# A new hand-written order for the same operations of a fused delta-rule and gated-MLP kernel

## The chip, the core and the metric

The kernel runs on one core of one Trainium2 chip. The metric is device time in microseconds (us), from the first to the last work of one execution. Five instruction queues work side by side: TensorE (PE in the profile, its weight loads PEld), VectorE (DVE), ScalarE (ACT), GpSimd (POOL) and the sync engine (SP), which here does nothing but issue DMAs. Each queue runs its instructions strictly in the order in which they were written; an instruction that waits holds up everything behind it on its queue.

## The reference

Two stages follow each other. The first is a delta-rule recurrence over 768 positions for 4 batches of 8 heads, head size 48:

```python
k_n = k / (np.linalg.norm(k, axis=-1, keepdims=True) + 1e-06)
for t in range(S):
    y[:, :, t] = np.einsum('bhd,bhde->bhe', q[:, :, t], state)
    v_old = np.einsum('bhde,bhd->bhe', state, kt)
    state = state + bt[:, :, :, None] * np.einsum('bhd,bhe->bhde', kt, vt - v_old)
```

Its output, with the heads side by side (384 wide), goes into a gated MLP:

```python
h = np.maximum(x @ w_in, 0.0)                    # 384 -> 1024
u, v = h[..., :512], h[..., 512:]
v_n = (v - mean(v)) / np.sqrt(var(v) + 1e-06)
v_s = np.einsum('ts,bsd->btd', w_spatial, v_n) + b_spatial[None, :, None]
return (u * v_s) @ w_out                         # 512 -> 384
```

## The kernel before

**The recurrence in steps.** Positions are taken in chunks of 64, and 24 steps `s` cover them (12 for the first two batches, 12 for the others). Within a chunk the recurrence is solved with a triangular inverse. `prep(g)` makes the inverses for four steps at once: matmuls of the keys with themselves (`kk`, line 557), a transpose into a layout with one system a lane (L576), norms (L584 to L591), and an elimination whose column steps are small elementwise operations, on DVE for groups 0 and 1 (L630, L633), on POOL for groups 2 to 5 (L615, L620); L645 transposes the result back. `widen16` and `widen` (L678 to L704 and L709 to L727; PE groups `e16`, `f16`, `e4`) put the small inverses together to 64 by 64. Then `step(s)` runs the chain that carries the state: PE group `a` (state times keys), a subtraction on DVE (L782), PE group `b`, a copy on ACT (L810, tile `w`), PE group `c`, and the update of the state on DVE (L823, L825 in step 0). `kq` (L753, its mask L757) and `qs`, `pu` make the output, which ACT copies to tile `xs` (L841). `load(s)` fetches k, q, v and n of a step (L733); there are two buffers `bn`, so the loads of step s+2 wait for the reads of step s.

**From the recurrence to the MLP.** After each two steps `convert(J)` moves six small pieces of `xs` by DMA (L858) and splits it into a high and a low part, `xh` on ACT (L862) and `xl` (L863, here on DVE), so that three products in a fast format make up one of full precision. `mlp(J)` then feeds PE with chunks of large matmuls (`v`, `u`), and `gate(b)` with the spatial and the output product (`g`, `o`).

**Decoding the weights.** w_in and w_out arrive as 64-bit floats. `load_f64` (L444) decodes a block: one load (L449), a chain of bit operations on ACT and DVE (L455 to L468), and a product, a difference and a sum (L469, L470, L471) that may run on DVE or POOL. There are six blocks `win0` to `win5`, all of which the MLP's first chunks need, and four blocks `wout0` to `wout3` that are needed much later.

**The order.** Nothing is scheduled by a tool when the kernel is built. `Plan.add` collects some 2,370 operations, and `listed` (L166) yields them in the order that the string `ORDER` spells out, two letters an operation; `PICK` has a digit for each operation that may run on either of two engines. A pair of letters beyond the last operation (`QW`) stands for a filler: two matmuls of a constant (`mpos`), whose result nobody reads; it is left out where no PSUM bank is free. `manual_schedule` keeps that order on each engine. All instructions of SP have line L411, all matmuls L524.

```python
for k in range(0, len(text), 2):
    i = LETTERS.index(text[k]) * n + LETTERS.index(text[k + 1])
    yield (self.ops[i], list(self.ops[i].alt)[pick.get(i, 0)]) if i < len(self.ops) else (None, None)
```

Of the kernel before, what the change touches and what calls it, by code (L numbers as in the profile page):

```python
# [36 lines left out]

LETTERS = "0123456789ABCDEFGHIJKLMNOPQRSTUVWXYZabcdefghijklmnopqrstuvwxyz!#$%&()*+-./:;<=>?@[]^_{|}~,"
ORDER = (
    "0407090605000102030J0Y080A0B0KQW0@0*0[QW0D0]0^0_0E0C0L0+0G0|0-0.0/0F0H0I0;1N0<1OQW1Y0N2U0M1P0P2R0:2S2V21221C2XQW2a0Q"  # L40
# [3 lines left out]
    "3L1p5U5V1J3M233H3N8R262P3B1A5Z3O451B3P1i1L1t1X1M2w2x2L2yQW2z2!2#2$3C2%3T2&3~2v2Q2(2)3U2*2+QW2-2.3D5X5Y5a3V3W3X3,403E"
    "QW3a413Y2/2:2;2<2=2>5b4L3Z463b42435c5d4447482?QW4A5e5f5g5h5i5j2@492[2]2^2_4M4N3I8U3eQW4O3i4B3kQW4CQW3h8d3j3d3l3c3f3g"
    "4P4QF74H4S4D4T4FQW5l2{5k5n2|1s5o5p5q2}3m4E4V4R4U4X4W4Y4G4Z4a4c5r8S5s8V2~8T5t515u5v5w8W5x4d5y525z1u1j5!4I3n4b504J1v4m"
    "536U3.3/3:4l5#3o565$4k4f4n4j4i4K4e8a5%8X5&1w1x556V5(5)5*5+5-575.5/3u1y5:1z5;5<5=3v3p5B3q5859546M5A3w5C3;3<6N3=6O5>5D"
    "6T5?3?1!6P3@6Q6R3r6W3[3s3]3^1#3t5@5[5]5^5_5F6j6S5m6X1%5E5{5G5|6k5}6l1$1&3x3y3z3>4o5~1(4h5,3_6Y6f6g1)6m6Z7O4p6a606d6n"
    "61623{6b8Y6c8Z5H6e5I3!5J6o3}1*QW3#631+647W8b7P8c7Q8e4q4g6q7X7R4:4]6566676p1-7S6r68694^4;6t6$4_4<3$1.3%3|8h3&7T6A6s6B"
    "1:6C6D6E6F6G6u7l7U6v6w6&6h6%3(6x1;8f8g4=4{6y4>6!6#6i6)6+6.6-6*6/7m7n1/4r7o4s6H6I6z8i7Y7t7p7h7q1=6J6K7s7V3)8j7r4?4t7u"  # L50
    "7Z6L8l8m4w4|4x7a7b4y7i7j6(8k3*8n8o6:8p8q6;7c7f7d8s4z4!7g9T7e8r9U4u4#4v7v7&8u4}7x4~8v8w8x8y7w7y78798z4@4,9V9q7)7(7A8!"
    "8#9a8$9W9r4[7z8%8&9X7!7$7*9s7%7k7+7/7-9Y1<7#At6]7B8(8)1>AV8*8+6^6_6<9b9t7C9c4$8-4%9u9v4&6=6>6?9y9dAu6{6|7D8.9Z3+9z8/"
    "8:8;9f9e8t4(9g9wAv6}8<8=9h7.7:IA7;9x9m1?9i9j6@9k7<4)9l1@7F6[8>4*8?Aw9!7G7H7IA>1[8@7E9#6~Ax8[Ay9$A?7J9%7=7_8]8^9&9*A@"
    "6,9+708_7>9nAz9p9o1]1^8{1|9(7?A#A[A]4+1_9)A!A%7@7[7]7{7|7}7^A^8|8QE~9/9.9@9-9>A$9?711{7K7L7NE{7M9=9<9;A(A|8}A&1}8~1~"
    "A)8A8,1,90A*3-7291928BAXA;A.A/8CA+8I7~8JQW8K8L8D8E8M8N8FA_A}7320AYAb939[A-9]7,7475A~9495AWAcAZ8P4-A{7680A,96Ad97B0AF"
    "9^B1AGAHAIB28O8HB39_A:B48182AaQWA<B5B6Ae984.999A9B9C9D9{AJAKE|9,9|9}A0F1BC4/E}83E,A1A284A3Af9~AgQWF0G5Ai9E85QWA48G9F"
    "9GBEBD9HF4BBBAGDB9B7A5A7Aj9IAhQW9J9K9L86A6AM9MGPGQG6ANAOAPAQF5ARASF29N9OF6Ak9PBFA8QW9QQWF3F8FAF99RF}BGBdGOFBFCBeF~Bf"
    "GH87A9QWF,ALFDG0GI9S88BNBOG1G2G4AAFFFGGJAUBPBQG|GKG3FEABG}G7BRA=ACGLG8FHAl9:B8FIGEFJFKBSADBgG9BHAmGMFMFNGAApGBGRG~GC"
# [1064 lines left out]
```

## Time and profile before

| | |
|---|---|
| Time, three runs | 472.31 us median (469.68 to 477.03) |
| Time of the profiled execution | 471.3 us, of which the span of its instructions is 469.6 us |
| First chunk of the MLP on PE | 85.5 us after the start |
| Fillers on PE | 24 before 109 us, 8 behind it |

The span starts with the first instruction of the program. A busy time is the union of the instructions' times on an engine. The profile also gives the clock that TensorE was granted, 1.0 for 2.4 GHz and 0.5 for 1.2 GHz.

### The profile page before, as it was taken

The numbers are of one execution on the slowest core, as the hardware profiler recorded it, in microseconds if no ns is written. First come the engines' busy times: TensorE is split into PE (matmuls) and PEld (weight loads), VectorE is DVE, ScalarE is ACT, GpSimd is POOL, SyncE is SP. The second block draws the span as 40 slices with busy tenths as digits, with TensorE's granted clock in tenths as the row PEclk, the third lists the DMA queues.
The fourth block names the chain that finished last, engine by engine and source line by source line (L and its number), as shares of the span: only waits on it lengthen the run. The fifth ranks groups of instructions, "written<-read, shape, count | busy, mean of one in ns | idle before, by whom it ended". The sixth has DMA issues, their size and how long they took to land.

```text
span 469.6 us, 21728 instructions
## 1 busy us (share of the span) xinstructions
PE 427.7 (91%) x9736; PEld 379.4 (81%) x9736; DVE 248.5 (53%) x558; ACT 230.6 (49%) x546; POOL 236.4 (50%) x371
## 2 busy tenths in 40 slices
...
GB/s 273 219 209 25 99 49 125 154 47 57 131 154 139 138 165 175 142 94 103 67 155 44 20 59 109 39 66 116 42 164 3 10 1 0 2 35 50 35 35 84
DMA packets 26109, 42.65 MB, mean 91 GB/s; under 512 B 4512, under 2 KB 14880, under 8 KB 26016
## 3 DMA queue, kind: packets, MB, share of 16 engines
...
## 4 chain that ended last, share of the span: by engine, by line
PE 81%; issue 5%; DVE 3%; ACT 3%; DMA 3%; SPq 2%; POOL 2%; ACTq 0%; DVEq 0%; POOLq 0%
PE ps L524 81%; SPq L411 2%; DMA bn<-in_k_t 2%; ACT xt L392 1%; DMA bn<-in_bun 1%; POOL ut L470 1%; POOL ut L469 1%; ACT w L810 1%; DVE la L576 0%; DVE xt L645 0%; DVE ut L464 0%; DMA xs<-xs 0%; DVE g L464 0%; ACT xs L841 0%; DVE pt L757 0%
## 5 line engine op out<-in xcount | busy, mean ns | idle before, releaser
L524 PE MATMUL ps<-wsph,vf 128*128 128x256 f32 x528 | 107.2, 285 | 0.0
L524 PEld LDWEIGHTS ps<-wsph,vf 128*128 128x128 f32 x528 | 86.6, 190 | 1.1
L620 POOL TENSOR_TENSOR wl<-wl,prod 128x60 f32<-128x60 f32 (+7 forms) x120 | 76.4, 636 | 9.1
L615 POOL TENSOR_TENSOR prod<-wl,la 128x60 f32<-128x60 f32 (+7 forms) x120 | 70.4, 586 | 9.3
L524 PE MATMUL ps<-wspl,vf 128*128 128x256 f32 x264 | 74.6, 283 | 0.0
L524 PEld LDWEIGHTS ps<-wspl,vf 128*128 128x128 f32 x264 | 50.3, 191 | 0.3
L980 DVE TENSOR_TENSOR gt<-ps,bbc 128x512 f32<-128x512 f32 x24 | 16.5, 689 | 52.6 <-PE ps L524 52.5
L524 PE MATMUL ps<-wout_h,g 128*128 128x384 f32 x128 | 35.2, 339 | 0.0
L392 ACT COPY xt<-xt 32x128 f32<-32x128 f32 (+1 forms) x85 | 29.3, 345 | 5.4 <-DVE xt L392 3.6
L524 PE MATMUL ps<-bn 64*64 64x64 f32 (+2 forms) x896 | 19.7, 232 | 9.7 <-DMA bn<-in_k_t 5.9
L983 POOL TENSOR_TENSOR gt<-gt,ut 128x512 f32<-128x512 f32 x11 | 15.1, 1372 | 25.4 <-DVE gt L980 25.3
L524 PEld LDWEIGHTS ps<-bn 64*64 64x64 f32 (+1 forms) x896 | 16.2, 139 | 13.4 <-issue 10.3
L810 ACT COPY w<-ps 128x384 f32<-128x384 f32 x24 | 11.5, 481 | 29.8 <-PE ps L524 29.8
L524 PE MATMUL ps<-mpos 128*128 128x256 f32 x64 | 24.8, 508 | 1.2 <-ACT xs L841 1.0
L985 ACT CAST g<-gt 128x512 fp32r<-128x512 f32 x16 | 9.9, 621 | 31.8 <-DVE gt L983 20.4
L524 PE MATMUL ps<-ke 64*64 64x64 f32 (+2 forms) x768 | 18.4, 254 | 6.7 <-ACT wl L642 3.3
L985 ACT CAST xt<-gt 128x512 fp32r<-128x512 f32 x8 | 5.0, 620 | 39.5 <-POOL gt L983 22.9
L524 PEld LDWEIGHTS ps<-ke 64*64 64x64 f32 (+1 forms) x768 | 15.6, 158 | 10.2 <-issue 4.0
L524 PEld LDWEIGHTS ps<-wout_h,g 128*128 128x128 f32 x128 | 22.9, 188 | 0.3
L757 DVE TENSOR_TENSOR pt<-ps,mpos 128x512 f32<-128x512 f32 (+1 forms) x27 | 16.6, 625 | 11.6 <-PE ps L524 11.3
L887 ACT ACTIVATE vr<-ps 128x512 f32<-128x512 f32 x22 | 13.1, 595 | 18.5 <-PE ps L524 18.3
L739 POOL TENSOR_TENSOR bn<-bn,nn 128x384 f32<-128x384 f32 x14 | 11.9, 854 | 20.0 <-DVE ps L633 5.1
...
## 6 DMA issues: line engine op xcount, KB each, us to landing
...
xs<-xs SPq DMA_DIRECT2D x66, 16.0 KB, 2.5
```

Source lines behind the costliest of these rows:

```text
L392: (nc.scalar.copy if e == "ACT" else ENG[e].tensor_copy)(out=out_, in_=in_)
L411: return P.add("SP", 0.39 if k.get("kb") else 0.57, lambda: nc.sync.dma_start(out=out_() if callable(out_) else out_, in_=in_() if callabl ...
L524: nc.tensor.matmul(o, l, r, start=start, stop=stop)
L615: P.add("POOL", cost, lambda: nc.gpsimd.tensor_tensor(out=pt if j else dst, in0=w3[:, :n, j : j + 1].broadcast_to([128, n, m]), in1=la3[:, ...
L620: P.add("POOL", cost, lambda: nc.gpsimd.tensor_tensor(out=dst, in0=dst, in1=pt, op=ALU.add), rd=["prod"], wr=[kw], pr=p0 + 2)
L739: P.add("", {"DVE": 0.56, "POOL": 0.83}, fn=lambda e: ENG[e].tensor_tensor(out=v, in0=v, in1=n.unsqueeze(3).broadcast_to([128, 2, 4, HD]), ...
L757: nc.vector.tensor_tensor(out=pt.rearrange("p (d a c) -> p d a c", d=2, a=2)[:, d], in0=v.rearrange("p d (a c) -> p d a c", a=2), in1=mpos ...
L810: P.add("ACT", 0.48, lambda: nc.scalar.copy(out=v3(w, 192), in_=v3(pc, 512)[:, :, 0:192]), rd=["pc"], wr=[("w", s % 2)], pr=pr)
L887: P.add("ACT", 0.69, lambda: nc.scalar.activation(out=raw_(r), in_=bank(h.unit), func=AF.Relu, accum_out=st[:, j : j + 1]), rd=[("pv", i)] ...
L980: P.add("DVE", 0.69, lambda: nc.vector.tensor_tensor(out=gt(), in0=v3(bank(h.unit), 256), in1=bbc[0][:, th * 256 : th * 256 + 256].unsquee ...
L983: P.add("", both(512), fn=lambda e: ENG[e].tensor_mul(out=gt_[t.unit], in0=gt_[t.unit], in1=u_(uh)[:, half * 512 : half * 512 + 512]), rd= ...
L985: P.add("ACT", 0.6, lambda: nc.scalar.copy(out=gv(gg)[0][:, hs], in_=gt_[t.unit]), rd=[kk], wr=[("gh", b, th, half)], pr=q)
```

## The change

Only the two strings change: the same 2,372 operations, with 36 fillers in the list in place of 34, in another order, and 50 operations moved between DVE and another engine or back.

```diff
 ORDER = (
-    "0407090605000102030J0Y080A0B0KQW0@0*0[QW0D0]0^0_0E0C0L0+0G0|0-0.0/0F0H0I0;1N0<1OQW1Y0N2U0M1P0P2R0:2S2V21221C2XQW2a0Q"
+    "090001QW0@0A02QW030407QW06050J0*0G0BQW0K0[0]0^0C0Y08QW0_0|0{QW0H0D0L0+QW0-0.0/0E241N0F0;0I2R2U1C220M1OQW0N0P2S2V1P0<"
...
 PICK = (
-    "00000111111100110111011100110010000000100000000000000011001100001100010000000000000000000010010011010010000010000000"
+    "10110111111100110111011100110110000000100000000000000011001100001100010000000000000000000010010011010100000000000000"
...
 )
```

Decoded, the queues differ as follows at the start (F is a filler, a number behind a name the step or chunk, `x(g)` the inverse of group g written back by L645).

```
PE before: kk0 kk3 F F kk1 kk2 F kk4 kk5 F F F F kk6 F F F F kk7 kq0 kk8 F kk9 F F
  e16.0 e16.1 f16.0 f16.1 e4.0 e4.0 e16.3 kq1 e16.2 F f16.2 kk10 b0 F e4.1 kk11 e4.1 f16.3 c0 F a1 F pu0 qs1
  b1 e4.2 F pu1 e4.2 c1 kq2 a2 F qs2 e4.3 F e4.3 b2 F F c2 kq3 pu2 F a3 qs3 b3 c3 pu3 kk12 kk13 e16.4 f16.4 kq4 u0 ...
PE after:  F F F kk0 F kk3 F F kk2 F kk1 F kk4 kk5 F F F F F kk7 kk6 F kq0 kk8 F F F kk9 F
  e16.0 e16.1 f16.0 F F kq1 e4.0 e4.0 f16.1 e16.2 e4.1 b0 e16.3 kk10 e4.1 f16.2 c0 F kk11 F F e4.2 pu0 e4.2 f16.3 F a1 qs1
  b1 e4.3 c1 kq2 e4.3 a2 pu1 kq3 qs2 b2 F c2 pu2 a3 qs3 b3 kk12 pu3 kq4 kk13 v0 e16.4 u0 u0 v6 v0 f16.4 v0 e16.6 v6 v6 e4.4 v6 e4.4 u0 ... c3
DVE before, from x(0) on: L645 L709 win3(L460 L462 L464 L467) win5:L460 L727 L709 win2:L460 L678 L576(group 1) ...
DVE after,  from x(0) on: L645 wout0:L460 L709 win5(L460 L462) wout0(L462 L464) win5:L464 L727 L678 L709
  win2:L460 win3:L460 wout0:L467 win3(L462 L464) win2(L462 L464) win3:L467 L727 L678 L576(group 1) ...
DVE before, end: ... L598 L633 wout0:L469 L823 L704 L757 L782 L645 wout0:L471 L863(xl of chunk 0)
DVE after,  end: ... L598 (8 of L630, L633) L823 L704 L757 L782 L645 L863(xl of chunk 0)
SP before: kk-loads k3 k0, win1 win0, k1 k2, win4 win5 ... then six L858 of chunk 0, with q, k, n of step 3 between them
SP after:  win1, k0 k3, win0, k2 k1 ... k, q of step 3, n and v of step 3, then six L858 of chunk 0
ACT before, chunk 1: ... win5:L459 ... L725 L700 ... L887 L948 L862(xh of chunk 1) L810
ACT after,  chunk 1: ... L841 wout1:L459 L563 L725 L862(xh of chunk 1) L700(widen of step 4) L702 L725 ...
```

Among the 50 changes of engine, three copies of `kk` results (L563, steps 0, 2 and 3) go from ACT to DVE, and the product of `wout0` (L469) from DVE to POOL. The rest lie behind the first MLP chunk.

## Rows read from the trace of the kernel before

**Rows 1.** The page: busy time of the engines; one group of DMAs.
```profile
PE 427.7 (91%) x9736; PEld 379.4 (81%) x9736; DVE 248.5 (53%) x558; ACT 230.6 (49%) x546; POOL 236.4 (50%) x371
...
xs<-xs SPq DMA_DIRECT2D x66, 16.0 KB, 2.5
```

**Rows 2.** Busy time by stretches: length, busy us (instructions), PEclk, DMA, GB/s.
```profile
0.00:81.41 81.41, 56.92 (x2132) 44.80 (x2133) 63.33 (x151) 44.20 (x97) 42.03 (x73) 0.75 0.45 142
...
85.50:469.60 384.10, 368.32 (x7486) 332.46 (x7482) 183.16 (x404) 185.08 (x447) 190.71 (x293) 0.98 0.26 80
```

The engines of Rows 2 and 3 stand in the order PE, PEld, DVE, ACT, POOL; the view's DMA is a busy share.

**Rows 3.** The same view, cut where the granted clock changes.
```profile
28.91:59.63 30.72, 23.30 (x924) 18.84 (x928) 26.72 (x64) 19.41 (x45) 15.27 (x20) 0.50 0.29 90
59.63:83.53 23.90, 16.26 (x776) 12.81 (x772) 17.11 (x38) 10.53 (x27) 15.74 (x31) 1.00 0.33 95
83.53:90.35 6.82, 6.82 (x174) 5.78 (x175) 3.58 (x5) 0.78 (x2) 6.11 (x10) 0.50 0.44 124
```

**Rows 4.** Waits of DVE, 13.7 to 81.4 us: total, times, longest.
```profile
DVE s L825 <- PE ps L524: 2.0, 1, 2.0
DVE pt L757 <- PE ps L524: 1.7, 1, 1.7
...
DVE bn L782 <- PE ps L524: 1.1, 1, 1.1
DVE s L823 <- ACT xt L392: 1.0, 1, 1.0
...
DVE s L823 <- PE ps L524: 0.7, 1, 0.7
```

**Rows 5.** Timeline of DVE: start us, us, line, operation, idle time before.
```profile
13.64 1.95 DVE L576 STREAM_TRANSPOSE la<-xt 128x1024 f32<-128x1024 f32 x1 [1.26 <-ACT xt L392]
...
17.63 1.18 DVE L589 TENSOR_TENSOR t<-nl 128x32 f32<-128x32 f32 x1
...
48.57 0.19 DVE L589 TENSOR_TENSOR t<-nl 128x32 f32<-128x32 f32 x1
...
77.33 2.11 DVE L645 STREAM_TRANSPOSE wspl<-wspl 128x1024 f32<-128x1024 f32 x1
...
80.08 1.32 DVE L863 TENSOR_TENSOR xl<-xs,xh 128x768 fp32r<-128x768 f32 x1
```

**Rows 6.** Timelines of POOL, of ACT and of SP's DMA issues.
```profile
17.48 1.28 POOL L469 TENSOR_TENSOR ut<-ut,vf 128x512 f32<-128x512 f32 x1 [12.17 <-ACT vf L466]
...
75.05 0.83 ACT L862 CAST xh<-xs 128x768 fp32r<-128x768 f32 x1 [2.19 <-DMA bn<-in_bun]
75.79 0.58 ACT L841 COPY xs<-ps 112x512 f32<-112x512 f32 x1
78.22 0.48 ACT L810 COPY w<-ps 128x384 f32<-128x384 f32 x1 [1.85 <-PE ps L524]
...
63.82 1.85 SPq L411 DMA_DIRECT2D xs<-xs  x3
...
69.25 1.06 SPq L411 DMA_DIRECT2D bn<-in_bun  x2
...
80.22 0.33 SPq L411 DMA_DIRECT2D g<-in_w_out  x1
```

**Rows 7.** Timeline of PE: start us, us, tiles, shapes, instructions, idle time before.
```profile
47.84 1.04 PE L524 MATMUL ps<-bn,xt 64*64 64x48 f32 x28
...
63.46 0.57 PE L524 MATMUL ps<-w,bn 64*48 64x48 f32 x32
...
74.36 0.69 PE L524 MATMUL ps<-bn 64*64 64x64 f32 x32 [2.62 <-DMA bn<-in_bun]
...
83.48 1.05 PE L524 MATMUL ps<-gi,bbc 16*32 16x16 f32 x64 [0.42 <-ACT gi L725]
84.46 1.13 PE L524 MATMUL ps<-bn 64*64 64x64 f32 x32
85.52 1.01 PE L524 MATMUL ps<-xh,win_h 128*128 128x256 f32 x3
```

More of the change, by code (lines that the diff above doesn't have):

```diff
@@ L44 @@
[L44 to L58, printed above, removed]
@@ new lines @@
+    "0:QW0!0#0$0%1k5K373G5N385L0~QWQW0>0,3Q101W0=0?QW365O0&2d23111Z2eQW260(281l1m271a1b1n1S2D291o1c5P122AQW2E2h1d1V2BQW2,"
+    "2C131E1q1F1G14151I3R30312f3233342g1p5M1H2F2I2G3J2i2k2l3S350)3K1K392N2t182m3L3A5Q5R2J5S1J161s2H172n1e2o2p2q1g2r5W3H3F"
+    "192j1f2u2s3M3N1r3O2K3BQW5T5U2O5V1L1MQW451h3P1t1i1A1B1X2w2LQW3~3,3D5a40412x3C2v2y2z2M2P2!2#2$2%2&2(2)QW3T3c5Y3E425X3V"
+    "3d8R2*5Z2+2-2Q4L2.2/3U2:5b3W3X4M4N3Y2;465c2<435d2=3Z474O483a3b4P3f3e3I1u5e8d5f4H5g5h444T4A2>495i5j4B5k2?2@2[2]2^4Q2_"
+    "2{2|4C5l4S5n5o5pQW5q5r5s4D5t5u2}5v4E5w4F4R5x4U5y4V4W4X3l4Y3g8S3i3k3j8U3h1j3m4Z4G4c4d2~3n5z4I1v1w5!8T6U8V3o515#5$6V1x"
@@ new lines @@
+    "8W505%525&4K3.3/5(3u3p4l4g4j4i5)53551y5*5+5-5.4J5/546M3q5B3v3w6N4m4k4n4o6O3x6P3:566T3y3;5:5;1z5<5=6Q57583<3=596j8X4a"
+    "6q5>5?5@3r6k3@3[3z1!1$5C6R5A4b6S1#5D3s6W3t3?6l5[1%QW3]6m3^5]3!5^3$3>5_3_6Y5G5F5m5E4p3{4q3|6n3}5H5{1&6X4r6Z6a6d5|1(5}"
+    "5~4f4e6f5,6g8a1)3#7W606e5I6o1*3%7X5J7O61626364656p1+661-674s8Y8b6b7P4t7Q8c7R4:7S6c6t6r7T6iE{6h681.8Z8e3&7U4;4u4h4<4="
+    "696s7l6v6$6u6w6&6%6A6B6C6D6E6F7m8h1;8g6x1:7n8f6y6(4w7o7p6G3(6H6z6I8i7q4v7V6J7s7r1=6K6L4x4>7Y7h6!4y4]6#8j6.6/6)7t6*6+"
+    "6-7u7Z8l8m4z4^4_7a7b7i7j4{4!8k3)8n8o8p8qIA7c7f8r7g7d4|4}8s9T6:7e8u6;8v4?9U4#4~4@4,4[9V7v7x7&6]7(6^8w8x9q7w4$8y8z1/9W"
@@ new lines @@
+    "9X1<8!8#8$3*4&4%QW6<7y6_6=6{9r1>7k1?7)F78%AV7z8&At4(7$7%6>7!8(9s4)9Y7;7+7*9a8)9b6?9t9u8*8+8-7#9c9Z3+9v8.8/8:8;786@6["
+    "799d9w9e7AAu9y7BQW9z9x9f8<9g7C6|9hAv1@7/7.E~7-7D7:6}7<A>4*9i8=9j1[8>6~9k8?9!7G9l7H7IAwAx7E4+9#1]QW9$9%8@7=8[9&7F8]8^"
+    "6,4-1^9p9m7_9(7>7?A?8_7J9*9o9-9/1|A@709+AyA[7K9n9=8Q9>9@9.9<7L7{A!8{9)4.1{1~8|8}8~8,Az90A#7|A%A]A^1_8tA$A_7191A&1}8I"
+    "7}8J7~A(7@7[7]927N7,93727MQW7^A|A)8K8L8A8MA*A;9;9?A.9[A/A}1,207394A+A{A-AXA:8N8B8CAYAb8DA~8E8FB08P8O74754/959]96A,80"
+    "9776B1AWAZ98Aa99B28GAc8HE|9^9_B39{9|9,8281AdE}9A9B9C9D9EB5A=9:B6A0A1E,B477F083GP9}A2A3B7AeAiAF9~9F84A4AGAf9GA5GQ9H9I"
@@ new lines @@
+    "9J9K9LG5AHAIF4F5AJAKA7AgAjBBF6ALG685AhAN9MA68687AkBCAOA<F1APAQARASF29NA8F3QW9OQW9P9Q9RBABEBDB9BFBGQWQWQWF}BdBeA9F9FA"
+    "88GD9SGOFBF8FCAUATAMB8AlF~GEBfF,G0BNG1GHBOBPGIBgBhFDAAFFAmFGG2GJFEABG3G4FHFIGKFJG7BQBRFKACG8ADG9ApGBGLAnGMAqGCG|GABH"
+    "FMBIFLGRG}BJGaBKGFGNGSG~BSBLBMFOFPFQGTFRArFSBTGUGVAoBiG,GWGYGcGGGbBlHJH0BUFTBVH~FUGZGgGfGjGiGdGhAsBWBXFVH1BmHKBnHLBo"
+    "BpGXH4FNFWBYBZFXI1H6BqHMHFGeH2BaH5FYHNFZH8BbBtBsBrBuBvBwBxFaFbH3FcH7FdHRH9ByBzFe89HOHPHABcBkGkHSB!HBB#B$FfHCFgFhFiHQ"
+    "FjFkB%B&B(B-HTB.B/B:B;B)B<B=B>B?B@GlBjB*B+HUB[B]FlHVFmHWHXB^H,HDB_HaHYB{HEHbFnHhGmB|I0B}B~B,C5C6C7C0C8C1C9CAC2HgHeHG"
@@ new lines @@
+    "HlGnHHHdHcCDFoCEFpFqFrFsFtFuFvFwAEC3CBFxFyFzF!F#F$F%F&F(CFCGCHCICJCKCLI2J9JAHZI3CMCNCOCTCUCVCWCXCYCZCaGoCbCcCdCeCPF)"
+    "F*CQCRI4I7F+CfHjI8I9C4HiF-F.CgCSJWJBHkJKCCI5ChI6IDIEICIBCiJXG+G-G.G/J0F/F:CjG:CrCsCkClCmCtCuCnCoCvCwF;F<F=F>F?F@F[F]"
+    "F^IFIGF_JVF{J8F|CxGpCpCzC!C#C$C%C&J1C(3-IHC)C*C+C-C.C=C>C?C@C[J2C]C^C_C{C|C}G;C/IIIJIKILIMINC:CqJOIOJ3G=C~G>DJG?GqJP"
+    "J4G@C,C;DNG<IPDKIRD0DTJQC<K3JCJ5D1ISD2GsGtGuG[GvK4JRG]GwDRDLGrJ6DPDSDUITIUDBG^DCD3G_D4D5D6DDDEDFD7DGD8IVIWIXJ7DQDMDO"
+    "IYIZIaIbIcJSK5G{JDHIIdJEJMJTD9DVDWJFHmDXJGK6JNDYK7DZDADaDbDcDdHnJUJHDeDfIeK8GxDHIfDgH@DlH[DmDnH]DoDpIgIhIiJYJhHfDhJI"
```

47 lines of the change are left out of this document (19 added, 28 removed).

## The prediction

> **What bounds the kernel now.** I read the page first, then busy time by stretches, the waits of DVE in the first stretch, and the timelines of DVE, SP and PE around the first chunk of the MLP; the two orders I decoded and laid side by side queue by queue. PE is busy 91% of the span [rows 1], but not evenly. From 85.5 us to the end it is busy 368.3 of 384.1 us at a mean clock of 0.98 [rows 2]: there PE is the bound, and only less work or fewer stalls on PE would shorten it. Before that, to 81.4 us, PE is busy 56.9 us at a mean clock of 0.75 [rows 2], mostly with small matmuls and fillers. That front ends with `xl` of chunk 0, at 80.08 + 1.32 = 81.4 us [rows 5], and PE starts the MLP at 85.52 [rows 7].
>
> What sets the front is DVE's queue. It is busy 63.3 of 81.4 us [rows 2], with 151 instructions in a row and little between them. From the first transpose at 13.64 [rows 5] to `xl` its longer waits sum to 6.5 us, in five places, 2.0 + 1.7 + 1.1 + 1.0 + 0.7, each time for the chain of the recurrence: the state of step 0, the mask of `kq`, the subtraction of step 3, and the states of steps 1 and 2 [rows 4]. The chain is late because weight decoding stands between its links, on DVE itself and on SP: `kq` of step 3 waits 2.62 us on PE for a load of `bn` [rows 7] that was issued at 69.25, behind the pieces of chunk 0, whose first three went out at 63.82 [rows 6].
>
> **The change, part by part.** Both queues hold almost the same DVE work up to `xl`; its order differs.
>
> *Start.* The first load is now `win1`, so DVE can start on it some us sooner. But the first L576 still needs all four `kk`, and the same five blocks of data lie ahead of the last of them in both orders. Three copies, as long as those on ACT, go to DVE ahead of it and fill the time gained. I take 0 for L576 at 13.64, with 1 us either way for the three fillers now ahead of `kk0`.
>
> *13.6 to 32.7 us.* The same DVE operations in nearly the same order: 0.
>
> *Step 0.* After `x(0)`, at 32.7 in both, DVE reaches L678 of step 0 with 8 operations ahead of it in place of 9, about 1 us sooner, and `b0` follows `e4.1` directly on PE, where before `f16.2` (with an L709 late on DVE) and `kk10` stood ahead of it as well. From L678, at about 36.4, two `e4`, `f16.1`, `e16.2` and `e4.1` lead to `b0`: five groups of at most 1.13 at 1.2 GHz and a copy on ACT between the first two, 6.1 us, so `b0` at about 42.5 to 43 in place of 47.84 [rows 7]. The state of step 0 is then no longer what DVE waits for: 2.0 us of its waits go. Between `c0` and `a1`, where one filler stood, are now four fillers and five groups, and the clock was 1.2 GHz here [rows 3]; so `a1` comes no sooner than it did (0).
>
> *Steps 1 to 3.* Between `b1` and `c1` stands one group of `e4` in place of three groups and a filler; and k and q of step 3 are issued as soon as step 1 has read them, ahead of chunk 0's pieces, so that they land some 6 us sooner than now. The waits 1.7, 1.1 and 0.7 end there. The wait of 1.0 for step 1 behind a busy ACT I expect to shrink to 0.5, and one of 0.9 to come at the subtraction of step 1, whose `a1` was not moved up. So of 6.5 us, 6.5 − 1.4 = 5.1 go. One product of `wout0` goes to POOL; a DVE operation of its size, 384 wide, is priced by the copy of that width on ACT, 0.48 [rows 6], so 0.5. `xl` then ends at 81.4 − 5.1 − 0.5 = 75.8.
>
> *The MLP's start.* On DVE, L645 (2.11) and `xl` (1.32) [rows 5] follow the subtraction of step 3, which is thus done at 72.4. PE then has `b3`, `kk12`, `pu3`, `kq4` and `kk13` ahead of the first `v0`: five groups of 0.57 to 0.69 [rows 7], together 3.2, so the MLP starts at 75.6 and not at 85.52: −9.9 us. Its first chunk needs `xh` alone.
>
> *Owed.* `c3`, `e16.4` and `f16.4` are done before 85.52 now and come after the start then. At 2.4 GHz `c` is 0.57 [rows 7]; `f16`, 1.05 at 1.2 GHz [rows 7], is half of that or a little more, and `e16` has as many small matmuls: +1.8.
>
> *A new wait.* ACT now has `xh` of chunk 1 ahead of L700 of step 4, for which the second `e4.4` waits on PE, and all PE work behind it. Step 3's `xs` is written at about 75.0 (`pu3`, then two copies of 0.58). Eight DMA issues at 0.5 [rows 6] and a landing of 2.5 [rows 1] put the pieces at 81.5, `xh` (0.83) [rows 6] and L700 end at 82.7. PE gets there after 12 groups, taken at 0.5 each (an estimate from the 0.57 of `c`), at 81.6: +1.1.
>
> *The rest of the list.* Behind that, I compared where each link of the chain stands among the PE groups: the same gaps within some groups, and the POOL elimination of groups 2 to 5 has the same or fewer foreign operations inside. The last 100 us are large matmuls on PE in both. The 46 other changes of engine lie beside a PE that is the bound; a POOL product of 1.28 [rows 6] in place of a shorter one on DVE costs nothing while PE has other chunks ahead, and less than 1.28 where it has not. I take 0, with 2 us either way.
>
> Sum: −9.9 + 1.8 + 1.1 = −7.0. The profiled execution took 471.3, so 464.3; the median before, 472.31, lies 1.0 above it.
>
> Two collisions stretch what I walked. A 32-wide product on DVE took 1.18 us at 17.63 while POOL ran a 512-wide one from 17.48 to 18.76, against 0.19 at 48.57 [rows 5, 6]. The Trainium skill (SBUF — State Buffer, "SBUF: two separate sides") says that the port pair which DVE and GpSimd share is held by one of them for a whole instruction and the other blocks; the trace agrees. By that rule, moving products to POOL would cost DVE up to 1.28 at each meeting. The meetings are as many in both orders, as far as the queues tell, so the sum holds none; one or two more of them are 1 to 2 us.
>
> **The rivals.** *More is gained.* PE ran at 1.2 GHz from 83.53 to 90.35, fully busy [rows 3], in the first us of the MLP, after a stretch in which it was busy only 16.3 of 23.9. After the change the groups before the MLP stand closer, and the clock may not fall: 6.8 / 2 = 3.4 us, and with it the waits that I left, 1.4: 464.3 − 4.8 = 459.5. For it speaks the denser queue, against it that only one filler stands between `b1` and the MLP, where there were six.
>
> *The clock eats it.* For just that reason PE may stay at 1.2 GHz, as from 28.9 to 59.6 [rows 3], up to the MLP. Ten groups on the chain from `c1` to `kk13` then take 1.13 in place of 0.69 (the two `kq` of rows 7): +4.4, so 468.7. The Trainium skill (TensorE: Matmul & The Clock Gate, "What's actually happening") says that the throttled state is the default and activity releases it; the fall at 83.53 in the trace agrees, and by that rule fewer fillers speak against this change.
>
> *Slower.* The load of `wout1` stands ahead of chunk 1's pieces on SP. Before, it left only at 80.22 [rows 6], when L471 had freed its tile, and SP stood still for it. Now L471 is earlier, but if SP is held again, `xh` of chunk 1 holds ACT, and with it all of PE. It decides from 7.0 us of delay on; if the pieces take what chunk 0's took, 63.82 to 75.05 [rows 6], 11.2 in place of the 6.5 assumed, and SP is held for 6 more, the loss is 4.7 + 6 = 10.7 and the time 464.3 + 10.7 = 475.0.
>
> *Nothing is moved.* That PE's total bounds all and the front is hidden anyway is excluded by PE's idle time there: 81.4 − 56.9 = 24.5 us [rows 2].
>
> **How the numbers follow.** The forecast 0.50, more gained 0.25, the clock 0.16, slower 0.09. The forecast's own range is 461 to 468 (start ±1, rest ±2, meetings). The whole range leaves out the low tail of the second case and most of the slower one: 458.5 to 471.5. Two per cent, about what a measurement of this kernel can tell from no change, is 461.9 against 471.3: the second case and a tail of the first lie below it, 0.27; beyond +2% lies only the far part of the slower case, 0.04; within, 0.69.
>
> **What would show it.** Right: `b0` near 43, `kq` of step 3 without a wait for its load, `xl` done near 75.8, the MLP on PE near 75.6, and from there to the end the same busy share. Wrong: L576 later than 14.6 (the start), the MLP later than 78 (a clock at 0.5 from 60 on, or waits of L823 and L825 that stayed), a wait of PE for L700 beyond 1.1, or idle time of PE beyond 100 us that was not there.

## The result, and the profile after

The changed kernel takes 469.32 us (median of 20 executions, 464.74 to 479.21), the kernel before 473.09 us (median of 20, 469.68 to 479.85). The ratio is 0.9905 with a 95% interval of 0.9877 to 0.9932: 4.5 us less, between 3.2 and 5.8. The time lies in the whole range of the prediction (458.5 to 471.5) and 1.3 us above the forecast's own (461 to 468); the difference is 2.5 us short of the 7.0 that the sum gave. The experiments show that most of it does not come from where the sum put it.

Single executions of one kernel differ by several us, and with them the mean clock that TensorE was granted: the new kernel's span was 463.0 us at a mean clock of 0.962 in one execution and 469.8 at 0.946 in another. So ratios give sizes here and profiles give places. The profiled execution of the new kernel took 469.2 us, that of the kernel before 471.3; among the experiments, the profiles of `e1_front_only` (476.9 us) and `e11_old_170_new_220_old` (473.2 us) are the longest executions of their kernels, so that what one of them alone shows is weaker.

The page of the new kernel, its line of busy times, which answers to [rows 1]: as many matmuls but for the fillers.

```profile
PE 429.4 (92%) x9742; PEld 380.0 (81%) x9742; DVE 254.8 (54%) x570; ACT 227.4 (49%) x539; POOL 236.0 (50%) x371
```

Busy time by stretches, up to the end of `xl` and from the first MLP chunk on (columns as in [rows 2]), and the stretches in which the granted clock changes (as [rows 3]):

```profile
0.00:77.70 77.70, 59.25 (x2026) 46.52 (x2030) 65.03 (x152) 41.43 (x90) 41.24 (x69) 0.74 0.48 153
79.65:467.50 387.85, 368.60 (x7644) 332.24 (x7644) 188.75 (x416) 184.45 (x446) 193.08 (x300) 0.99 0.26 79
...
57.20:70.90 13.70, 9.43 (x504) 7.65 (x497) 11.81 (x33) 7.63 (x20) 7.42 (x11) 1.00 0.42 129
70.90:77.70 6.80, 6.53 (x216) 6.00 (x220) 5.53 (x10) 2.38 (x4) 5.65 (x13) 0.50 0.56 173
77.70:90.00 12.30, 11.05 (x429) 8.08 (x422) 4.98 (x10) 3.62 (x8) 11.00 (x17) 1.00 0.37 110
```

From the first MLP chunk to the end 387.85 us pass, where it was 384.10 [rows 2]: of the 5.8 us by which the MLP starts sooner in these two executions, 3.75 are gone at the end. The clock is at 0.5 from 70.90 to 77.70, just ahead of the MLP, and not behind its start as before [rows 3].

Waits of DVE from 13.7 us to the end of `xl`, which answer to [rows 4] (the wait of 2.4 is the one ahead of the first L576):

```profile
DVE la L576 <- ACT xt L392: 2.4, 1, 2.4
DVE s L823 <- PE ps L524: 0.9, 1, 0.9
DVE bn L782 <- PE ps L524: 0.7, 1, 0.7
DVE xt L727 <- PE ps L524: 0.5, 1, 0.5
DVE xt L727 <- ACT xt L392: 0.5, 1, 0.5
```

The timelines of DVE, of PE and of ACT (as [rows 5 to 7]): L576, L645 and `xl`; then on PE the part of `kk1` behind its stop, `b0`, `a1`, the part of `e4.3` behind its stop, `kq3`, `b3` and the first MLP chunk; then `xh` of chunk 1.

```profile
15.34 1.95 DVE L576 STREAM_TRANSPOSE la<-xt 128x1024 f32<-128x1024 f32 x1 [2.44 <-ACT xt L392]
...
74.61 2.13 DVE L645 STREAM_TRANSPOSE wspl<-wspl 128x1024 f32<-128x1024 f32 x1
76.63 1.07 DVE L863 TENSOR_TENSOR xl<-xs,xh 128x768 fp32r<-128x768 f32 x1
```

PE and ACT:

```profile
13.73 0.89 PE L524 MATMUL ps<-bn 64*32 64x64 f32 x48 [2.80 <-issue]
...
44.96 1.10 PE L524 MATMUL ps<-bn,xt 64*64 64x48 f32 x32
...
59.04 0.68 PE L524 MATMUL ps<-s,bn 48*64 48x48 f32 x32
...
65.60 0.39 PE L524 MATMUL ps<-xt,pi 32*32 32x32 f32 x25 [2.07 <-issue]
...
66.87 0.65 PE L524 MATMUL ps<-bn 64*64 64x64 f32 x32
...
74.75 1.11 PE L524 MATMUL ps<-bn,xt 64*64 64x48 f32 x32
...
79.69 0.73 PE L524 MATMUL ps<-win_h,xh 128*128 128x512 f32 x2 [0.24 <-ACT xt L392]
...
85.93 0.83 ACT L862 CAST wsph<-xs 128x768 fp32r<-128x768 f32 x1 [3.86 <-DMA xs<-xs]
```

The wait of L825 for step 0 is gone, `kq3` waits for nothing, and `xl` ends at 77.70 (75.8 forecast, 81.4 before). But the MLP starts at 79.69 and not at 75.6, and two stops of PE stand in the way for which the profile names no releaser: 2.80 us within `kk1` and 2.07 within `e4.3`.

### The profile page after: what moved, and what is told of

Same layout as the page of the kernel before. It is cut to its first block, busy times and chain, and to the rows that moved or that the text cites. A ratio compares the mean times of both kernels' runs of the same rounds, so it can differ in the third digit from the quotient of the medians.

```text
span 467.5 us, 21742 instructions
## 1 busy us (share of the span) xinstructions
PE 429.4 (92%) x9742; PEld 380.0 (81%) x9742; DVE 254.8 (54%) x570; ACT 227.4 (49%) x539; POOL 236.0 (50%) x371
## 4 chain that ended last, share of the span: by engine, by line
PE 80%; issue 5%; ACT 5%; DVE 5%; DMA 2%; SPq 1%; ACTq 0%; DVEq 0%
PE ps L524 80%; ACT xt L392 1%; SPq L411 1%; DMA xs<-xs 1%; DMA bn<-in_k_t 1%; DVE ps L633 1%; DVE prod L630 1%; ACT wspl L392 1%; ACT ut L945 0%; DVE la L576 0%; ACT w L810 0%; ACT xh L862 0%; DVE ut L464 0%; DVE pt L757 0%; ACT gt L897 0%
## 5 line engine op out<-in xcount | busy, mean ns | idle before, releaser
L620 POOL TENSOR_TENSOR wl<-wl,prod 128x60 f32<-128x60 f32 (+7 forms) x120 | 75.4, 628 | 9.3
L615 POOL TENSOR_TENSOR prod<-wl,la 128x60 f32<-128x60 f32 (+7 forms) x120 | 70.8, 590 | 10.2 <-DVE ps L633 1.1
L524 PE MATMUL ps<-wout_h,g 128*128 128x384 f32 x128 | 34.1, 338 | 0.0
L524 PE MATMUL ps<-mpos 128*128 128x256 f32 x70 | 27.4, 523 | 3.0 <-POOL mpos L433 3.0
L983 POOL TENSOR_TENSOR gt<-gt,ut 128x512 f32<-128x512 f32 x7 | 9.0, 1291 | 40.3 <-DVE gt L980 40.3
L757 DVE TENSOR_TENSOR pt<-ps,mpos 128x512 f32<-128x512 f32 (+1 forms) x31 | 16.8, 564 | 17.2 <-PE ps L524 17.1
L823 DVE TENSOR_TENSOR s<-s,ps 112x384 f32<-112x384 f32 x20 | 11.0, 550 | 27.4 <-PE ps L524 23.1
L524 PE MATMUL ps<-bn 64*64 64x64 f32 (+2 forms) x896 | 18.6, 226 | 5.5 <-issue 2.8
L1001 ACT COPY ob<-ps 128x384 f32<-128x384 f32 x24 | 11.0, 480 | 24.1 <-PE ps L524 17.1
L841 ACT COPY xs<-ps 112x512 f32<-112x512 f32 (+1 forms) x24 | 12.9, 550 | 18.7 <-PE ps L524 18.6
```

The costliest lines, as they stand in the source:

```text
L524: nc.tensor.matmul(o, l, r, start=start, stop=stop)
L615: P.add("POOL", cost, lambda: nc.gpsimd.tensor_tensor(out=pt if j else dst, in0=w3[:, :n, j : j + 1].broadcast_to([128, n, m]), in1=la3[:, ...
L620: P.add("POOL", cost, lambda: nc.gpsimd.tensor_tensor(out=dst, in0=dst, in1=pt, op=ALU.add), rd=["prod"], wr=[kw], pr=p0 + 2)
L757: nc.vector.tensor_tensor(out=pt.rearrange("p (d a c) -> p d a c", d=2, a=2)[:, d], in0=v.rearrange("p d (a c) -> p d a c", a=2), in1=mpos ...
L823: P.add("DVE", 0.55, lambda: nc.vector.tensor_tensor(out=sv, in0=sv, in1=pv, op=ALU.add), rd=["pc"], wr=["S"], pr=pr)
L841: nc.scalar.copy(out=x.rearrange("p (d q t) -> p d q t", d=2, q=4)[0:KR, d, :, s % 2 * 64 : s % 2 * 64 + 64], in_=v[0:KR].rearrange("p d ( ...
```

## What the unnamed stops are

The front was sized from DVE's queue. PE's own waits were not read there, and the largest of them are put down to "issue": 7.4 us in 8 stops up to 85 us before, 8.2 us in 8 stops up to 80 us after. Counting the matmuls that PE had begun when such a stop came shows what they have in common. Busy time of the kernel before, from 0 to the beginning of three of its stops (the first number in brackets is PE's count):

```profile
0.00:11.00 11.00, 5.11 (x222) 3.95 (x223) 4.91 (x11) 5.30 (x8) 4.44 (x19) 1.00 0.76 268
0.00:65.28 65.28, 45.51 (x1623) 35.84 (x1623) 51.58 (x124) 37.71 (x81) 31.54 (x51) 0.69 0.47 152
0.00:81.45 81.45, 56.96 (x2132) 44.80 (x2133) 63.37 (x151) 44.24 (x97) 42.07 (x73) 0.75 0.45 142
```

The same of the new kernel, where other groups stand at the first two counts (`kk1` in place of `kk2`, `e4.3` in place of `a2`; the third is in `e16.4` in both):

```profile
0.00:10.92 10.92, 7.77 (x222) 5.41 (x223) 6.84 (x13) 4.61 (x6) 5.74 (x20) 1.00 0.78 263
0.00:63.50 63.50, 48.77 (x1623) 37.35 (x1624) 53.23 (x124) 35.51 (x76) 32.73 (x50) 0.73 0.47 154
0.00:80.65 80.65, 61.73 (x2132) 48.35 (x2133) 66.94 (x156) 42.96 (x93) 43.88 (x73) 0.75 0.46 148
```

The counts are the same: 222, 1,623 and 2,132. Between them lie 11 times 127.4 and 4 times 127.3 matmuls. The 14 traces of this case have 137 stops of PE longer than 0.7 us that are put down to "issue", and every one begins within 6 matmuls of 222 plus a multiple of 127.4. The page's list of DMA queues has a queue that carries instructions:

```profile
q8 instruction: 76, 1.25, 1.1%
```

76 packets of 16,384 bytes for 9,742 matmuls and as many weight loads, one packet for about 128 pairs. The Trainium skill (Trainium Architecture — The Big Picture, "The software stack") says that an instruction has 64 bytes; the trace agrees, with 16,384 / (2 x 127.4) = 64.3. In the trace of the new kernel such a packet begins at 11.18 and at 63.38 us and takes 1.02 and 0.97 us, and PE goes on at 13.73 and 65.60, 1.5 and 1.3 us after it has arrived. Over the 14 traces of this case the closest two packets are 3.26 to 3.47 us apart in each; from 30 to 90 us they come 3.85 us apart on average in the new kernel and 4.14 in the kernel before.

So the theory that I then held against my own: between about 30 and 110 us, where PE has mostly small matmuls, it cannot take 127 of them in less than some 3.3 us, whatever their order and whatever DVE does. The groups of 32 last 0.57 to 0.69 us [rows 7], four of them 2.3 to 2.8. A new order of the same matmuls then moves PE little by its count of matmuls, even if the first MLP chunk, which is earlier in the new list, comes sooner. Two things keep this a theory: the averages of 3.85 and 4.14 us lie above 3.3, so the packets are not the only limit of this stretch, and no run made them come faster.

## The experiments

Every kernel is made of the two lists; "new" and "old" are the lists of the changed kernel and of the kernel before. Times are differences to the kernel before on the same chip, worked out from the ratio and its interval.

**Which part of the list gains.** The first three runs join the lists at a point.

```diff
 e1_front_only:   new up to the first MLP chunk (80 us)
-                 new behind it
+                 old behind it
 e2_rest_only:
-                 new up to the first MLP chunk
+                 old up to the first MLP chunk
                  new behind it
 e3_new_then_old: new up to 220 us
-                 new behind it
+                 old behind it
```

> The new order up to the first MLP chunk on PE, then every other operation in the order (and on the engines) of the kernel before. Theory A, the front gives the gain: in the profile of the new kernel PE starts the MLP 5.8 us sooner and owes 1.8 us of groups; so 3 to 4 us below the kernel before, first MLP chunk at 79 to 80 us. Theory B, the gain comes from the list behind the front and PE's later stalls swallow whatever the front gives: within 1 us of the kernel before, although the MLP starts at 79 to 80 us.

Measured: ratio 0.9999 (0.9962 to 1.0035), so 0.0 us, between 1.8 less and 1.7 more. The MLP starts at 78.29, but PE then has `c3`, `e16.4` and `f16.4` ahead of the next chunk, as the old list wants it, and these took from 78.95 to 84.81, with the clock at half from 83.10 to 90.00. Timeline of PE:

```profile
78.29 0.73 PE L524 MATMUL ps<-win_h,xh 128*128 128x512 f32 x2 [0.25 <-ACT xt L392]
...
84.81 1.01 PE L524 MATMUL ps<-xh,win_h 128*128 128x256 f32 x3 [2.96 <-issue]
```

Its busy time up to 85 us:

```profile
0.00:85.00 85.00, 60.03 (x2261) 46.93 (x2262) 69.00 (x159) 43.70 (x95) 49.07 (x81) 0.81 0.46 148
```

In this execution the stop of 2.96 us comes when 2,260 matmuls have begun, again a multiple of 127.3 behind 222 (16 of them). At 85 us PE has begun 2,261 matmuls here, 2,242 in the kernel before and 2,260 in the new one. Theory A is wrong: the front by itself gains nothing that can be measured.

> The opposite half: the order of the kernel before up to the first MLP chunk, then the order and the engines of the new kernel. Theory A: within 1 us of the kernel before (its new list gains about 3 us around 180 to 200 us and gives about 3.5 us back from 290 to 330 us, as the two traces show). Theory B: 4 us below the kernel before. Both: first MLP chunk at 85 to 86 us.

Measured: 0.9955 (0.9914 to 0.9996), 2.1 us less (0.2 to 4.1), first MLP chunk at 85.77. Between the two theories: the rest of the list, for which the sum had 0, gains.

> The new order up to about 220 us (the first 1,243 entries), then every other operation in the order of the kernel before. In the two traces the new kernel is 5 to 6 us ahead from 220 to 290 us and 2 us ahead from 360 us on. Theory: the new list itself loses these 3 to 4 us (stalls of PE of 1.3 and 1.6 us at steps 19 and 21 and a fall of the clock at 320 us), so this kernel keeps the lead: 6 to 7 us below the kernel before, no fall of the clock at 320 us. Rival: the stalls there come with any order and only fall elsewhere: 4 to 5 us below, as the new kernel.

Measured: 0.984 (0.9783 to 0.9896), 7.6 us less (4.9 to 10.2), a median of 464.62 us. Busy time of one stretch, in the new kernel:

```profile
290.00:330.00 40.00, 36.76 (x904) 33.04 (x904) 15.33 (x31) 13.48 (x36) 22.75 (x44) 0.96 0.25 74
```

And here:

```profile
290.00:330.00 40.00, 38.73 (x890) 35.19 (x891) 15.30 (x36) 16.21 (x42) 23.84 (x39) 1.00 0.21 66
```

PE is busy 2.0 us more of the 40, at a clock that does not fall. In the new kernel the stop ahead of the fall at 320 us is 1.63 us long, in `e4.21`, and "issue" again; here a stop comes at the same count of matmuls, 7,996, and is 0.81 us long. So the new list gives some 3 us back behind 220 us. The intervals of the two kernels (3.2 to 5.8 and 4.9 to 10.2) overlap a little, so this rests on the traces as much as on the times. It has the lowest ratio of the study, though the intervals of e4, e6 and e12 reach into its own.

> The new order up to about 120 us (the first 624 entries), then the order of the kernel before. The same cut at 80 us gave no gain, the cut at 220 us 7.6 us. Theory A, the gain is made between 80 and 120 us, where the new list puts the small groups of steps 3 and 4 between MLP chunks one by one: 4 us below the kernel before or more. Theory B, it is made at step 12 (180 to 200 us): within 1.5 us of the kernel before.

```diff
 e5_new_to_120: new up to 120 us
-               new behind it
+               old behind it
```

Measured: 1.0035 (0.9996 to 1.0075), 1.6 us more (from 0.2 less to 3.5 more). This does not tell the theories apart, for the cut itself cost something: the pieces of chunk 2 land late, `xh` of chunk 2 waits for them on ACT, and `pu6` on PE waits for tile `w`, which stands behind `xh` on ACT. Timelines of ACT and of PE:

```profile
128.64 0.83 ACT L862 CAST xh<-xs 128x768 fp32r<-128x768 f32 x1 [3.93 <-DMA xs<-xs]
...
129.90 0.95 PE L524 MATMUL ps<-pt,w 64*48 64x64 f32 x32 [3.98 <-ACT w L810]
```

It is the prediction's slower rival in another place: a late piece holds ACT, and ACT holds PE, for 3.98 us.

> The kernel before, with the new list only for what lies between about 170 and 220 us (steps 10 to 14); the order before on both sides. Theory, the gain of the new list is made there, where the kernel before stops PE twice ahead of e4.12 and e4.13 and its clock falls: 3 to 4 us below the kernel before, no stop at e4.12. Rival, the gain comes of what was gathered before 170 us: within 1 us.

```diff
 e11: old up to 170 us
-     old from 170 to 220 us
+     new from 170 to 220 us
      old behind it
```

Measured: 0.9931 (0.9889 to 0.9973), 3.3 us less (1.3 to 5.2), as the theory has it. The place can be read off. Kernel before, around the transpose of group 3 (L645), timelines of DVE, ACT and PE:

```profile
188.25 2.17 DVE L645 STREAM_TRANSPOSE xt<-wl 128x1024 f32<-128x1024 f32 x1
...
189.85 0.59 ACT L392 COPY xt<-ps 128x512 f32<-128x512 f32 x1 [0.17 <-PE ps L524]
190.47 2.50 ACT L392 COPY xt<-xt 32x512 f32<-32x512 f32 x4
...
193.63 0.36 ACT L700 ACTIVATE pi<-ps 128x256 f32<-128x256 f32 x1
...
194.05 0.45 PE L524 MATMUL ps<-xt,pi 32*32 32x32 f32 x32 [1.14 <-ACT pi L700]
195.35 0.45 PE L524 MATMUL ps<-tn,xt 32*32 32x32 f32 x32 [0.85 <-DVE tn L678]
```

The same of `e11_old_170_new_220_old`:

```profile
192.94 0.69 DVE L392 COPY xt<-ps 128x512 f32<-128x512 f32 x1 [1.47 <-PE ps L524]
193.55 2.15 DVE L645 STREAM_TRANSPOSE xt<-wl 128x1024 f32<-128x1024 f32 x1
...
193.67 2.51 ACT L392 COPY xt<-xt 32x512 f32<-32x512 f32 x4 [0.20 <-DVE xt L392]
...
197.46 0.45 PE L524 MATMUL ps<-xt,pi 32*32 32x32 f32 x32 [0.22 <-ACT pi L700]
```

Before, the copies of the next group's `kk` (2.50 us on ACT) stood between the first `e4.12` and L700, which the second `e4.12` needs. In the new list the last of the wide copies is one of the 46 changes of engine and runs on DVE ahead of L645, and the four short ones run on ACT while L645 does. PE's stop for L700 shrinks from 1.14 to 0.22, the one for L678 ends, and the clock, which fell to 0.5 from 196.2 to 199.6 us before, stays. From L645 to `b12` pass 200.0 - 188.3 = 11.7 us before and 201.1 - 193.6 = 7.5 here; in the new kernel, 191.7 - 184.1 = 7.6. The 4.2 us that this chain gains are read from the traces; the run carries the whole new list from 170 to 220 us, so its 3.3 us are not those of the copies alone.

> The kernel before up to the first MLP chunk, the new list up to about 220 us, the order before behind that: e3_new_then_old without its front. The difference from e3 is the worth of the front. If the front is worth what the prediction's sum says (8.1 us at the MLP's start, with what it owes): within 1 us of the kernel before. If it is worth its lead in matmuls issued, about 2 us: 5 to 6 us below. If nothing: 7 to 8 us below.

```diff
 e12: old up to the first MLP chunk
-     old up to 220 us
+     new up to 220 us
      old behind it
```

Measured: 0.9887 (0.9825 to 0.9949), 5.3 us less (2.4 to 8.3), as the theory of about 2 us for the front wants it; but the interval reaches to the figure of "nothing" too. Only the prediction's 8.1 is out.

**Whether DVE, the clock or the packets hold the front.**

> The new kernel with five more fillers on PE, behind b1, c1, the second e4.3, qs2 and c2. Theory, the clock is what the MLP's start lacks: the clock stays at 1.0 from 57 us on, the groups from c2 to kk13 lose the 3.2 us by which half clock stretches them, the fillers cost 0.70 us each, of which some lie in stalls: first MLP chunk at 77.5 to 79 us in place of 79.7, and 5 to 6 us below the kernel before. Rival, PE's queue is full there and each filler delays the chain: first MLP chunk at 81 to 83 us, 2 to 3 us below the kernel before.

```diff
 new:  ... b1   e4.3   c1   kq2 e4.3   a2 pu1 kq3 qs2   b2 F c2   pu2 ...
+e4:   ... b1 F e4.3   c1 F kq2 e4.3 F a2 pu1 kq3 qs2 F b2 F c2 F pu2 ...
```

Measured: 0.988 (0.9812 to 0.9948), 5.7 us less (2.5 to 8.9); the first MLP chunk at 79.29. Busy time of the stretch in which the clock is up:

```profile
55.50:76.00 20.50, 15.89 (x677) 12.08 (x666) 16.27 (x41) 8.53 (x22) 12.60 (x24) 1.00 0.46 143
```

Timeline of PE, the first MLP chunk:

```profile
79.29 0.77 PE L524 MATMUL ps<-win_h,xh 128*128 128x512 f32 x2
```

The clock does stay at 1.00 to 76.00 and not to 70.90, and yet the MLP starts 0.4 us sooner and no more. Single profiles differ by more than that: the new kernel, e1, e3 and e5, with one and the same list up to the first MLP chunk, start it at 79.69, 78.29, 78.59 and 79.86; the old list starts it at 85.31 to 85.77 in four traces, and at 88.92 in that of e11. And five fillers at 0.70 us cost 3.5 us, about the 3.4 that the prediction puts on 6.8 us at half clock. So fillers buy the clock at about its price, and the run does not exclude that the half clock holds the MLP's start back. PE's stops for "issue" from 55 to 80 us are 3.0 us here and 3.7 in the new kernel. The expected time was met, the expected start was missed by 0.3 us. The same five fillers in the kernel of e3 bring nothing that repeats:

> The kernel of e3_new_then_old with the five fillers of e4_five_fillers. If what the fillers hold up (the clock ahead of the MLP) and what the old list holds up behind 220 us add up: 8 to 9 us below the kernel before. If the clock ahead of the MLP is worth nothing: 7 to 7.6 us below.

Measured: 0.9915 (0.9866 to 0.9963), 4.0 us less (1.7 to 6.3), where e3 without them has 7.6; first MLP chunk at 79.78. Neither figure expected was met; the gains do not add up.

> The kernel of e3_new_then_old with two of the four fillers between c0 and a1 left out, and a1, b1, c1 and a2 with their subtractions and state updates moved ahead of the groups of e4 that stand before them. Theory A, the prediction's step that a1 comes no sooner was what held the front: a1 at 54.5 in place of 57.3, the state of step 1 at 61 in place of 63, first MLP chunk at 76 to 77 in place of 78.6 us, and 1 to 2 us less in all. Theory B, PE is held from 32 to 78 us by the arrival of its own instructions (one packet of 16,384 bytes for some 127 matmuls, 3.3 to 3.6 us apart at the closest): a1 comes sooner, but PE is at the same count of matmuls at the same time, and the first MLP chunk stays within 1 us of 78.6.

```diff
-PE of e3: c0 F kk11 F F e4.2 pu0 e4.2 f16.3 F a1 qs1 b1 e4.3 c1 kq2 e4.3 a2 ...
+PE of e6: c0 F kk11 a1 e4.2 pu0 qs1 b1 e4.2 f16.3 F c1 kq2 a2 e4.3 e4.3 ...
```

Measured: 0.9882 (0.9846 to 0.9918), 5.6 us less (3.9 to 7.3). Timeline of PE:

```profile
53.33 1.10 PE L524 MATMUL ps<-s,bn 48*64 48x48 f32 x32
```

Busy time up to 85 us:

```profile
0.00:85.00 85.00, 65.84 (x2259) 52.12 (x2260) 67.04 (x158) 42.98 (x94) 46.13 (x77) 0.74 0.46 146
```

`a1` starts at 53.33 and not at 57.3, 4.0 us sooner, and the MLP starts at 80.39, 1.8 us later than in e3. Theory A falls. Theory B's figure (within 1 us of 78.6) is missed as well, by 0.8, and so is its count against e3, from which this kernel is made: 2,259 matmuls at 85 us against 2,308. The new kernel and e5, with the list of e3 up to there, have 2,260, so the run does not settle theory B.

> The kernel before with one thing changed: the loads of k and q of step 3 are issued as soon as step 1 has read them, ahead of the pieces of chunk 0. By the prediction's sum the wait of kq3 (2.6 us) and the wait of 1.7 us on DVE behind it go: first MLP chunk at 83 in place of 85.5 us, 2 us less in all. By the theory of the packets PE is at most 1 us ahead by its count of matmuls at 85 us and the time is within 1 us of the kernel before.

```diff
 SP before: ... L541(ke1)  v of step 3  L858 L858 L858 ... q of step 3  L858  k of step 3 ...
+SP of e10: ... k of step 3  q of step 3 ... L541(ke1)  v of step 3  L858 L858 L858 ...
```

Measured: 0.9976 (0.9932 to 1.0021), 1.1 us less (from 3.2 less to 1.0 more). The wait of `kq3` for its load is gone, as the prediction said, and so is the 1.7 at L757; but DVE now waits longer for PE one step earlier. Waits of DVE from 13.7 to 80 us:

```profile
DVE s L823 <- PE ps L524: 3.5, 2, 3.2
```

L823, which waited 0.7 and 1.0 [rows 4], waits 3.2 once. `xl` ends at 79.5, but the first MLP chunk is at 84.95, 0.6 us sooner than before, and PE has begun 2,255 matmuls at 85 us, 2,242 before. By these the late load was a real wait that cost little; the interval of the time reaches to the 2 us of the prediction's sum and to nothing.

> The new kernel with each filler as eight matmuls of 64 columns in place of two of 256: the same columns, six more matmuls in each, some 160 more ahead of the MLP. Theory, PE is held by the arrival of its instructions there: 160 / 127 = 1.3 more packets at 3.4 us each, so the first MLP chunk 3 to 5 us later (83 to 84 us), and PE's longer stops at the same counts of matmuls (223, 1624, 2133) as in every kernel so far. Rival, a filler costs what its columns cost: first MLP chunk within 1 us of 79.7, stops at other counts.

```diff
-    P.filler = lambda u: mm(bank(u)[:, 0:256], mpos, mpos.unsqueeze(1).broadcast_to([128, 2, 128]))
+    P.filler = lambda u: [mm(bank(u)[:, 64 * j:64 * j + 64], mpos, mpos[:, 0:64]) for j in range(4)]
```

Measured: 1.0302 (1.0231 to 1.0373), 14.2 us more (10.9 to 17.6), first MLP chunk at 96.58. Both theories miss, because a filler's price was not its columns, and because PE ran at 1.2 GHz up to 82 us. Busy time up to there, and a timeline of PE with a filler and a group `b` on either side:

```profile
0.00:82.00 82.00, 76.09 (x1792) 71.77 (x1792) 53.72 (x125) 36.51 (x78) 33.70 (x52) 1.00 0.37 120
...
74.33 1.97 PE L524 MATMUL ps<-mpos 128*128 128x64 f32 x8
...
78.17 1.11 PE L524 MATMUL ps<-bn,xt 64*64 64x48 f32 x32
...
84.96 0.67 PE L524 MATMUL ps<-bn,xt 64*64 64x48 f32 x32
85.56 1.10 PE L524 MATMUL ps<-mpos 128*128 128x64 f32 x8
```

The 1.00 of the first line is not a clock that was granted: the trace's first record of the clock is at 82.3 us, and the view counts the time ahead of it as full. The groups tell what ran: `b` took 1.11 us at 78.17 and 0.67 at 84.96, as in the new kernel at half clock (1.11 at 74.75) and at full (0.67 at 69.59). In the other traces the first record comes at 6.0 to 8.9 us, in e9 at 19.6, so mean clocks of stretches that begin at 0, those of [rows 2] among them, are a little high.

At one clock, a filler of eight matmuls of 64 columns took 1.97 us at 1.2 GHz and 1.10 at 2.4; one of two matmuls of 256 columns, as many in all, took 1.22 (at 14.55) and 0.70 (at 58.41) in the new kernel. So the run does not measure the packets. Two things of it are of use: PE's longest "issue" stop behind 85 us, 1.81 us, comes after 2,006 matmuls, 14 times 127.4 behind 222; and up to 80 us, where PE was slow, its "issue" stops sum to 0.4 us, against 8.2 in the new kernel. The Trainium skill (TensorE: Matmul & The Clock Gate, "What's actually happening") says that activity releases the throttle; this trace does not bear that out for busy time, for PE was busy 76.09 of 82.00 us and its groups were as long as at 1.2 GHz.

> The kernel before with 768 matmuls of 32 by 32 (and their 768 weight loads) added behind everything else, which nothing waits for and which wait for nothing. Theory, PE gets its instructions in packets of 16,384 bytes, one for some 127 matmuls, no closer than 3.3 us apart: the 768 matmuls take some 6 x 3.4 = 20 us, with a stop of PE of 1 to 2 us every 127 matmuls. Rival, the stops have another cause (semaphores, the data's DMA): nothing moves data there, so the 768 run without a stop, in 768 x 14 to 20 ns = 11 to 15 us (the price of one in the groups of e4 and kq).

```diff
     with tc.manual_schedule():
         P.emit()
+        for j in range(384):
+            mm(bank(0)[0:32, 0:32], mpos[0:32, 0:32], mpos[0:32, 0:32])
```

One execution. Timeline of PE:

```profile
466.10 38.41 PE L524 MATMUL ps<-mpos 32*32 32x32 f32 x768
```

Busy time of that stretch:

```profile
466.00:504.60 38.60, 38.50 (x769) 38.27 (x768) 0.00 (x0) 0.48 (x1) 0.00 (x0) 0.55 0.04 13
```

No stop, but no test of the stops either: one after another on the same corner of the array they took 50 ns each, so 127 of them 6.4 us, and a packet every 3.3 us is in time for that. The least distance of two packets thus rests on the 14 traces, not on an experiment made for it. What a packet holds is shown, though, by the page's line of the instruction queue:

```profile
q8 instruction: 82, 1.34, 1.1%
```

6 packets more than the 76 of the kernel before came with 768 matmuls and 768 weight loads more: 256 instructions a packet.

## Why the prediction was right, and where it was not

The difference, 4.5 less, lies within what the forecast's own range allows (3.3 to 10.3 less), but by two errors that partly cancel, so the hit is in part luck. Of the front's 7.0 us about 0 to 2 are there, and the rest of the list, put at 0, gains about 5 up to 220 us and gives about 3 back behind it.

- **Start, 0 with 1 us either way: right in six traces of seven.** L576 begins at 15.34 in the profile of the new kernel, behind the stop of 2.80 us in `kk1` and beyond the 14.6 that was to show the step wrong, and at 13.49 to 14.24 in the six other traces with this start.
- **Step 0: right in kind.** `b0` comes at 44.96 (42.5 to 43 forecast), at 43.10 to 43.79 in the six others, and DVE's 2.0 for L825 is gone.
- **`a1` no sooner: it is 2.9 us later**, 59.04 against 56.1, behind fillers at half clock. By e6 that does not matter: with `a1` 4.0 us sooner the MLP did not start sooner.
- **DVE's waits 6.5 to 1.4:** four waits of 0.5 to 0.9, 2.6 in all, are left, and `xl` ends 1.9 us later than forecast.
- **The MLP's start, -9.9: the step that failed.** It is -5.8, with the start at 79.69, beyond the 78 that was to show it wrong; and even that is mostly the list, in which the first MLP chunk now stands ahead of three groups. The subtraction of step 3 was done at about 74.6 and not 72.4, and the five groups behind it, from 74.75 to 79.69, took 4.9 us at mostly half clock and not 3.2 (3.7 in e3, where the clock was up). The sum let PE follow DVE. PE's own stops for its instructions were in the profile of before, as 7.4 us of "issue" among its waits, and I did not read that view. By the count of matmuls PE is about where it was: 2,242 at 85 us before, 2,260 after; and in e1 the front alone gains 0.0 us, at most 1.8. That the stops for instructions are the reason is argued, not shown: they come to 8.2 us up to 80 us in the new kernel, 7.5 in e3, 4.4 in e4 and 5.0 in e6, and the MLP starts at 79.69, 78.59, 79.29 and 80.39, not sooner where they are fewer.
- **Owed, +1.8: too small by kind.** The same three groups took 5.9 us in the profile of e1, of which 3.9 were stops. In the new list they are spread between MLP chunks, and there they cost no stop of more than 0.91 us.
- **The new wait at L700, +1.1: not there.** `xh` of chunk 1 came at 85.93, 4 us later than I reckoned, since its pieces landed late, but PE reached `e4.4` only at 86.69 and did not wait for it. That the mechanism exists is shown by e5, where the same order of ACT cost 3.98 us.
- **The rest of the list, 0 with 2 either way: wrong on both sides.** The list from 170 to 220 us, with its changes of engine and of ACT's order around step 12, is worth 3.3 us (e11), all from the first MLP chunk to 220 us 5.3 (e12), and the list behind it gives some 3 back (e3). "Beside a PE that is the bound" failed at step 12 because PE there waits for one chain: L645, L678, `e4`, L700, `e4`.
- **The rivals.** The clock did fall ahead of the MLP, from 70.90 to 77.70, as that rival said, and its 2.6 us less are as near to the 4.5 measured as the forecast's 7.0. e4 does not exclude it, for there the fillers that kept the clock up cost about what it gives. "More is gained" held in one point, the clock does not fall in the MLP's first us, and SP was not held by the load of `wout1`.

What stays open: how much of the front's 0 to 2.4 us (e1 by itself; e2 against the new kernel; e12 against e3) is real, for the intervals are as wide as that; whether the packets, the half clock or both hold the front; and what makes the packets come when they come.
